# Columns of a modulation matrix by VectorE sums, low parts of early x tiles on GpSimd, and statistics' rows two tiles at a time, in a fused attention and mixer block

## The chip, the core and the metric

The kernel runs on one core of a Trainium2 chip, alone. The metric is the device time of one execution in microseconds (us). Engines are named as in the profile: PE (TensorE's matmuls, with PEld for its weight loads), DVE (VectorE), ACT (ScalarE), POOL (GpSimd), SP (the queue that issues most DMAs).

## The reference, cut to what matters

The input x has 2048 tokens of D = 448 channels; c is one row of 448 and w_mod is 448 x 2688.

```python
mod = (_silu(c) @ w_mod).reshape(c.shape[0], 6, 1, -1)
sa, ca, ga, sb, cb, gb = (mod[:, 0], mod[:, 1], mod[:, 2], mod[:, 3], mod[:, 4], mod[:, 5])
h = _layernorm(x, axis=-1) * (1 + ca) + sa
x = x + ga * _A_ref(h, A_wqkv, A_wo)     # linear attention: phi(k)^T v, then phi(q) times it, times wo
h = _layernorm(x, axis=-1) * (1 + cb) + sb
x = x + gb * _B_ref(h, B_w1, B_b1, B_w2, B_b2)   # layernorm, gelu MLP over the tokens
```

The change concerns the first layernorm with its scale `1 + ca` and shift `sa`, and the K projection behind it.

## The kernel before, in words

Tokens are cut into 16 tiles of 128 (t = 0 to 15), channels into four chunks of 128, 128, 128 and 64 (ch = 0 to 3; the last chunk is stored twice, in partitions 0 to 63 and 64 to 127). The order of the instructions on each engine is the order in which the program is written; a manual schedule is switched on, and semaphores are put in between engines.

A float32 product is made of float32r products of a rounded high part and the remaining low part. For tile t, `xt` is x transposed. ACT copies it into `hh` (`a_split_high`, L406), DVE subtracts to get `hl` (`a_split_low`, L409). The weights are scaled on the way: `1 + ca` is needed as a column, one number per channel on the partitions. ACT multiplies a chunk of the raw K weights `wr` by it into `wh` (`w_high`, L256), DVE makes the low part `wl` (`w_low`, L268). A tile's K projection `kp` is ten matmuls (`project`, L426): hh with wh, hh with wl, hl with wh for chunks 0 to 2, and hh with wh for chunk 3, where the doubled halves carry the low part. An eleventh matmul (`close`, L433) brings in the mean of the token and the shift: it uses rows that a small transpose (`a_transpose`, L399, tile `rw`) makes of the token statistics, which DVE lays out in `rowst` (`a_rows`, L389 and L391) and ACT copies into `hl` (`a_copy`, L402), and a weight row `wrow` (`row_out`, L290 and L291), which needs the sums of the scaled weights (`row_sum`, L283) and of the weights times `sa` (`row_part` on DVE, L274 and L276, into `accb`; `row_bias`, L286).

The columns come from `w_mod` in its own layout, channels of c on the partitions. For `1 + ca` (j = 1) two chunks are multiplied by silu(c) on PE (`col_mm`, L218 and L220), the others first weighted on DVE (`col_acc`, L204 to L211) and then summed by PE; `col_out` (L226) takes the column out of PSUM. For `sa` (j = 0) DVE weights all four pieces, PE sums once.

Statistics: for tiles 0 to 3 ACT makes the sums (L357, L336), for the others DVE does (`BN_STATS`, L373, and `BN_AGGR`, L374); GpSimd raises the variance to the powers 1/2 and -1/2 (L348, tile `mv`). The exp and relu of K on ACT (L440, L441), phi on DVE (`pk`, L446), its parts (`pkh` L504, `pkl` L506 or L508), the normalised x (`xn` L484, `xh` L488, `xl` L494) and the outer products (`cacc`, L530, eleven matmuls a tile) follow. From t = 4 on this is one loop; in an iteration t the parts of tile t + 3 are made, tile t + 1 is projected, and the outer product of tile t - 4 is added.

What the first 40 us wait for is loaded in the written order by SP; a DMA is issued when the one eight places earlier has landed.

Of the kernel before, what the change touches and what calls it, by code (L numbers as in the profile page):

```python
# [14 lines left out]
P = 128  # L15
# [13 lines left out]
RING = 6  # L29
# [3 lines left out]
DVE_LOW = (0, 1, 13, 14, 15)  # L33
# [8 lines left out]
WARM = 9  # L42
# [8 lines left out]
def block_kernel(ctx: ExitStack, tc: tile.TileContext, x, xt, wqkv, wo, w1, b1, w2, b2, c, wmod, wfirst, out):  # L51
# [47 lines left out]
    cst.tile([P, 40], F32, name="space")  # L99
# [19 lines left out]
    c_sb = cst.tile([P, 8], F32, name="c_sb")  # L119
    nc.sync.dma_start(c_sb, c)  # L120
# [12 lines left out]
    wm = {}  # L133
# [6 lines left out]
    raw_w = {}  # L140

    def load_qkv(j, new=None, chs=range(4)):
        new = new or slot
        for ch in chs:
            raw_w[j, ch] = new(f"wr{j}_{ch}")
            nc.sync.dma_start(raw_w[j, ch], wqkv[j, ch])

    def load_first(j):
        for k in range(4):
            w = D if k < 3 else 256  # L150
            wm[j, k] = slot(f"wm{j}_{k}", w)
            nc.sync.dma_start(wm[j, k], wfirst[j, :, k * D:k * D + w])
# [16 lines left out]
    load_qkv(0)  # L169
    load_xt(6)  # L170
    load_x(6)
    for t in (7, 8):
        load_xt(t)
        load_x(t)
# [11 lines left out]
    ec = cst.tile([P, 8], F32, name="ec")  # L186
    nc.scalar.activation(ec, c_sb, AF.Exp, scale=-1.0)
    sc = cst.tile([P, 8], F32, name="sc")
# [10 lines left out]
    one = ones[:, 0:1]  # L199

    def col_acc(j):
        acc = macc[j] = slot(f"acc{j}")
        if j:
            nc.vector.tensor_scalar_mul(acc, wm[j, 2], sc[:, 2:3])  # L204
        else:
            nc.vector.tensor_scalar_mul(acc, wm[j, 0], sc[:, 0:1])
            for k in (1, 2):
                nc.vector.scalar_tensor_tensor(acc, wm[j, k], sc[:, k:k + 1], acc, op0=ALU.mult, op1=ALU.add)
        for r, (c0, c1) in enumerate(((0, 256), (256, D))):
            p = slice(r * 64, (r + 1) * 64)  # L210
            nc.vector.scalar_tensor_tensor(acc[p, c0:c1], wm[j, 3][p, :c1 - c0], sc[p, 3:4], acc[p, c0:c1],  # L211
                                           op0=ALU.mult, op1=ALU.add)

    def col_mm(ps, a, b, first, last):
        b = b.to_broadcast([P, P])
        for ch in range(4):
            n = P if ch < 3 else 64
            nc.tensor.matmul(ps[:n, ch * P:(ch + 1) * P], a[:, ch * P:ch * P + n], b, start=first and ch == 0,  # L218
                             stop=last, skip_group_check=True)
        nc.tensor.matmul(ps[64:, 384:512], a[:, 384:D], b, start=False, stop=last, skip_group_check=True)  # L220

    def col_out(j, ps):
        col[j] = cst.tile([P, 4], F32, name=f"col{j}")
        ps = ps.rearrange("p (c n) -> p c n", n=P)[:, :, 0]
        if j == 1:
            nc.vector.tensor_scalar_add(col[j], ps, 1.0)  # L226
        else:
            nc.vector.memset(col[j], 0.0)
            nc.vector.tensor_copy(col[j][:, :3], ps[:, :3])
            nc.vector.tensor_copy(col[j][:64, 3:4], ps[:64, 3:4])  # L230

    def mod_part(j, k):
        if k == 0:
            macc[j] = (tslot if j == 5 else slot)(f"acc{j}", parts=G)
            nc.vector.tensor_scalar_mul(macc[j], wm[j, 0], sc[:G, 4:5])
        else:
            nc.vector.scalar_tensor_tensor(macc[j], wm[j, k], sc[:G, 4 + k:5 + k], macc[j], op0=ALU.mult, op1=ALU.add)
# [93 lines left out]
    heads, mv, xn = {}, {}, {}  # L331
# [18 lines left out]
    def a_stats_act(ts):  # L350
# [10 lines left out]
        def end():  # L361
            nc.gpsimd.tensor_scalar_mul(g[:, :, 0:1], sm[:, :, 0:1], 1.0 / D)
            nc.gpsimd.tensor_scalar(ve, sm[:, :, 2:3].to_broadcast([P, n, 2]), 1.0 / D, EPS,
                                    op0=ALU.mult, op1=ALU.add)
            a_pow(g, ve)
        return one, end

    def a_stats_dve(ts):
        g, ve = a_group(ts)

        def one(i):
            b6 = small.tile([P, 6], F32, name=f"st{ts[i]}", tag="st")
            nc.vector.bn_stats(b6, X[ts[i]])  # L373
            nc.vector.bn_aggr(mv[ts[i]][:, 0:2], b6)  # L374
# [4 lines left out]
        return one, end  # L379

    def a_stats(t):
        one, end = a_stats_dve((t,))
        one(0)
        end()

    def a_rows(t):
        r = rowst[t % RING]
        pair = mv[t][:, 0:2]
        nc.vector.tensor_copy(r[:, 64:].rearrange("p (b c) -> p b c", b=2)[:, :, 0:2],  # L389
                              pair.unsqueeze(1).to_broadcast([P, 2, 2]))  # L390
        nc.vector.tensor_sub(r[:, 66:68], pair, r[:, 64:66].bitcast(F32))  # L391
# [3 lines left out]
    def a_transpose(t0, n=1):  # L395
        ps = bank(f"rw{t0}")
        for i in range(n):
            tps[t0 + i] = ps[:, i * P:(i + 1) * P]
            nc.tensor.transpose(tps[t0 + i][:ROWS], rowst[(t0 + i) % RING][:, :ROWS].bitcast(F32), ident)  # L399

    def a_copy(t):
        nc.scalar.activation(heads[t][1][64:ROWS, 384:], tps.pop(t)[64:ROWS], AF.Copy)  # L402
# [5 lines left out]
    def a_split_low(t):  # L408
        nc.vector.tensor_sub(heads[t][1], XT[t], heads[t][0].bitcast(F32))  # L409
        XT[t] = None  # L410
# [27 lines left out]
    def a_exp(t, ps):  # L438
        eks[t] = (slot(f"ek{t}"), slot(f"rk{t}"))
        nc.scalar.activation(eks[t][0], ps, AF.Exp, scale=mv[t][:, 2:3])  # L440
        nc.scalar.activation(eks[t][1], ps, AF.Relu, scale=mv[t][:, 2:3])  # L441
# [79 lines left out]
    def a_outer(t):  # L521
# [4 lines left out]
        for ch in range(4):  # L526
            s = slice(ch * P, (ch + 1) * P)
            todo = [(xh, kh), (xh, kl)] + ([(xl, kh)] if ch < 3 else [])
            for i, (a, b) in enumerate(todo):
# [3 lines left out]
    pc = bank("col1")  # L533
    for k in range(2):
        col_mm(pc, wm[1, k], sc[:, k:k + 1], k == 0, False)
    nc.scalar.activation(sel_s, sel_f, AF.Copy)
    col_acc(1)
    a_split(0)
    col_mm(pc, macc.pop(1), one, False, True)
    keep_warm(5)  # L540
    col_out(1, pc)
    for ch in (3, 0, 1, 2):
        w_high(1, ch)
        w_low(1, ch)
    a_split(1)
    a_split(2)
    projects([(0, "hh", 0), (0, "hl", 0), (0, "hh", 3), (0, "hh", 1), (0, "hl", 1), (0, "wl", 0), (0, "hh", 2),
              (0, "hl", 2), (0, "wl", 1), (1, "hh", 0), (1, "hh", 1), (1, "hh", 2), (1, "hh", 3), (0, "wl", 2),
              (1, "wl", 0), (1, "wl", 1), (1, "wl", 2), (1, "hl", 0), (1, "hl", 1), (1, "hl", 2)], 1, "kp")
# [38 lines left out]
    project(4, 1, "kp")  # L588
    a_split(5)
    a_low(0)  # L590
    kps = [close(t, 1) for t in (0, 1)]
    a_transpose(2, 2)
    project(5, 1, "kp")
    a_exp(0, kps[0])
    a_pk(0, kps[0])
    dve45(1)
# [4 lines left out]
    a_exp(1, kps[1])  # L601
    a_norm(1)
    a_pk_parts(0)
    a_outer(0)
    a_pk(1, kps[1])
    a_rows(4)
    a_rows(5)
    a_transpose(4, 2)
    a_exp(2, kps[2])
    a_split_high(6)  # L610
    a_pk(2, kps[2])
    a_split_low(6)
# [6 lines left out]
    a_stats(6)  # L619
    a_pk_parts(1)  # L620
    a_low(1)
    a_rows(6)
    a_pk(3, kps[3])
    a_pk_parts(2)
    a_stats(7)
    wo_sb = []
    late = [t for t in range(NT) if t not in Q_EARLY.values()]
    for t in range(4, NT):
# [3 lines left out]
        if 4 < t < NT - 1:  # L632
            a_transpose(t + 1)
# [3 lines left out]
        if t > 4:  # L637
            a_outer(t - KV_LAG)
        if t in Q_EARLY:
# [3 lines left out]
        if 4 < t < NT - 2:  # L643
            a_rows(t + 2)
        if 5 <= t < 9:
            w_low(0, t - 5)
            row_part(0, t - 5)
        if 7 < t + 3 < NT:
            a_stats(t + 3)
        a_phi_q(t in Q_EARLY)  # L650
        if 4 < t < NT - 1:
            a_copy(t + 1)
        a_exp(t, kp)
# [4 lines left out]
        for i in highs[:1]:  # L658
            a_norm(i)
            a_high(i)  # L660
        a_pk(t, kp)
        if t + 3 < NT:
            a_split_low(t + 3)
        for i in highs[1:]:
            a_norm(i)
            a_high(i)
        for i in highs:
            a_low(i)
        if 4 <= t < 8:
# [564 lines left out]
def lay_out(inputs):  # L1234
# [12 lines left out]
    col = np.zeros((P, 8), c.dtype)  # L1247
    for k in range(3):
        col[:, k] = c[k * P:(k + 1) * P]
    col[:64, 3] = col[64:, 3] = c[3 * P:]  # L1250
    for k in range(4):
        col[:G, 4 + k] = c[k * G:(k + 1) * G]
    a['c'] = col
    a['B_wmod'] = a['w_mod']
    first = np.zeros((2, P, 3 * D + 256), c.dtype)
    for j in range(2):
        m = a['w_mod'][:, j * D:(j + 1) * D]
        for k in range(3):
            first[j, :, k * D:(k + 1) * D] = m[k * P:(k + 1) * P]
        first[j, :64, 3 * D:] = m[3 * P:, :256]  # L1260
        first[j, 64:, 3 * D:3 * D + 192] = m[3 * P:, 256:]
# [25 lines left out]
```

## Time and profile before, and how to read them

| what | value |
|---|---|
| median of 3 runs | 441.46 us (440.39, 441.46, 441.61) |
| the profiled execution: its time, and its span | 440.71 us, 439.0 us |
| PE busy | 433.3 us (99% of the span) |
| DVE busy | 364.0 us (83%) |
| ACT busy | 279.4 us (64%) |
| POOL busy | 118.2 us (27%) |
| granted TensorE clock | 1.00 in all stages |

The profile is of one execution. The span counts from its first to its last instruction; 1.7 us of the time lie around it. A row of the timeline gives start, duration, engine, source line, operation and tiles, how many instructions are merged in the row, and in brackets how long the engine had been idle and for whom. A row of the chain of waits gives start, duration, engine, tile and line; the chain is followed back from the last instruction to whatever released it. A row of the stages gives each engine's busy time in the stretch, the clock, the share of DMA time and the GB/s. In the groups, the first figure after the bar is the sum in us, the second the mean in ns.

### The profile page before, as it was taken

The numbers are of one execution on the slowest core, as the hardware profiler recorded it, in microseconds if no ns is written. First come the engines' busy times: TensorE is split into PE (matmuls) and PEld (weight loads), VectorE is DVE, ScalarE is ACT, GpSimd is POOL, SyncE is SP. The second block draws the span as 40 slices with busy tenths as digits, with TensorE's granted clock in tenths as the row PEclk, the third lists the DMA queues.
The fourth block names the chain that finished last, engine by engine and source line by source line (L and its number), as shares of the span: only waits on it lengthen the run. The fifth ranks groups of instructions, "written<-read, shape, count | busy, mean of one in ns | idle before, by whom it ended". The sixth has DMA issues, their size and how long they took to land.

```text
span 439.0 us, 7315 instructions
## 1 busy us (share of the span) xinstructions
PE 433.3 (99%) x2383; PEld 401.3 (91%) x2383; DVE 364.0 (83%) x822; ACT 279.4 (64%) x598; POOL 118.2 (27%) x200
## 2 busy tenths in 40 slices
PE   8999999999999999999999999999999999999996
PEld 7878899999899999999999999999999999999996
DVE  3989998689889999995579785829799988898894
ACT  3899877657676698885765263627555555655550
POOL 3137554300004567783300000010112231132010
PEclk9999999999999999999999999999999999999999
DMA  7997999545410025534616661579379987985430
GB/s 244 385 311 162 220 227 246 95 140 187 127 30 1 24 50 135 105 74 96 193 61 199 204 189 45 145 206 234 59 182 229 193 183 156 225 171 125 85 52 32
DMA packets 64085, 66.17 MB, mean 151 GB/s; under 512 B 4976, under 2 KB 55600, under 8 KB 64048
## 3 DMA queue, kind: packets, MB, share of 16 engines
q1 hardware_dynamic: 55120, 51.17, 38.3%
q0 software_dynamic: 8928, 14.55, 21.0%
q8 instruction: 18, 0.29, 0.3%
q14 instruction: 19, 0.16, 0.1%
HBM read 46.11 MB, written 7.34 MB: 122 GB/s over the span
## 4 chain that ended last, share of the span: by engine, by line
PE 96%; DVE 1%; ACT 1%; issue 0%; ACTq 0%
PE y L1077 19%; PE up L860 10%; PE up L861 10%; PE up L862 10%; PE y L1078 9%; PE op L810 8%; PE cacc L530 8%; PE qp L426 7%; PE kp L426 6%; PE tq L785 1%; PE col L218 1%; PE warm L181 1%; PE qp L433 1%; PE kvb L741 1%; PE rowb L283 1%; PE wp L877 1%
## 5 line engine op out<-in xcount | busy, mean ns | idle before, releaser
L860 PE MATMUL up<-h2h,ph 128*128 128x448 f32 x224 | 81.3, 363 | 0.0
L862 PE MATMUL up<-h2h,pl 128*128 128x448 f32 x224 | 81.1, 362 | 0.0
L861 PE MATMUL up<-h2l,ph 128*128 128x448 f32 x224 | 80.9, 361 | 0.0
L1032 POOL DMA_DIRECT2D a<-a x16 | 14.2, 963 | 139.4 <-DMA pr<-in_B_w_dram 75.3
L862 PEld LDWEIGHTS up<-h2h,pl 128*128 128x128 f32 x224 | 42.0, 188 | 3.1
L861 PEld LDWEIGHTS up<-h2l,ph 128*128 128x128 f32 x224 | 41.9, 187 | 3.1 <-DVE h2l L857 0.3
L860 PEld LDWEIGHTS up<-h2h,ph 128*128 128x128 f32 x224 | 42.0, 188 | 2.5
L83 DVE TENSOR_TENSOR pl<-pr,ph 128x512 fp32r<-128x512 f32 x46 | 30.8, 688 | 4.1 <-ACT ph L82 3.3
L1083 ACT ACTIVATE cc<-y 128x448 f32<-128x448 f32 x24 | 13.0, 546 | 26.8 <-PE y L1078 26.8
L82 ACT ACTIVATE ph<-pr 128x512 fp32r<-128x512 f32 x46 | 27.6, 624 | 0.8 <-PE up L862 0.5
L996 DVE TENSOR_TENSOR u<-u,mod 128x448 f32<-128x448 f32 x14 | 8.7, 623 | 21.6 <-ACT u L995 21.4
L530 PE MATMUL cacc<-pkh,xh 128*128 128x448 f32 x64 | 24.4, 382 | 0.3 <-ACT pkh L504 0.3
L810 PE MATMUL op<-wph,pth 128*128 128x448 f32 x64 | 24.5, 383 | 0.0
L995 ACT ACTIVATE u<-up,b1c 128x448 f32<-128x448 f32 x14 | 8.8, 625 | 24.1 <-PE up L862 23.5
L530 PE MATMUL cacc<-pkl,xh 128*128 128x448 f32 x64 | 23.3, 364 | 0.2 <-DVE pkl L506 0.2
L426 PE MATMUL kp<-wh,hh 128*128 128x448 f32 x64 | 23.2, 373 | 0.2 <-ACT wh L256 0.2
L426 PE MATMUL qp<-wh,hh 128*128 128x448 f32 x64 | 23.3, 364 | 0.0
L810 PE MATMUL op<-wpl,pth 128*128 128x448 f32 x64 | 23.1, 362 | 0.0
L1097 POOL DMA_DIRECT2D out_dram<-yt x14 | 12.5, 893 | 39.1 <-DVE yt L1088 29.7
L767 POOL TENSOR_SCALAR den<-den 128x16 f32<-128x16 f32 x16 | 8.8, 549 | 47.7 <-DVE den L764 47.7
L348 POOL TENSOR_TENSOR mv<-ve,roots 128x2 f32<-128x2 f32 (+1 forms) x13 | 12.5, 960 | 22.4 <-DVE ve L377 21.6
L1038 DVE TENSOR_TENSOR a<-a,s 128x512 f32<-128x512 f32 (+1 forms) x32 | 18.5, 619 | 0.0
(238 smaller groups left out, 1382.7 us busy)
## 6 DMA issues: line engine op xcount, KB each, us to landing
pr<-in_B_w_dram SPq DMA_DIRECT2D x56, 256.0 KB, 3.3
a<-in_B_w_dram SPq DMA_DIRECT2D x32, 256.0 KB, 4.8
a<-in_B_w_dram SPq DMA_DIRECT2D x32, 192.0 KB, 4.6
xt<-in_xt_dram SPq DMA_DIRECT2D x16, 256.0 KB, 4.9
x<-in_A_x_dram SPq DMA_DIRECT2D x16, 224.0 KB, 4.8
wm<-in_B_wmod_dram SPq DMA_DIRECT2D x16, 196.0 KB, 4.8
out_dram<-x SPq DMA_DIRECT2D x14, 224.0 KB, 2.2
out_dram<-yt POOLq DMA_DIRECT2D x14, 224.0 KB, 6.3
```

The costliest lines, as they stand in the source:

```text
L82: nc.scalar.activation(hi, full, AF.Copy)
L83: nc.vector.tensor_sub(lo, full, hi.bitcast(F32))
L426: nc.tensor.matmul(pps[t, j][:, :D], a[:, ch * P:(ch + 1) * P], w, start=first, stop=False)
L530: nc.tensor.matmul(cacc[ch][:, :D], a[:, s], b, start=(t == 0 and i == 0), stop=(t == NT - 1 and i == len(todo) - 1))
L810: nc.tensor.matmul(opb[t][:, :D], a, b, start=(n == 0), stop=(n == len(todo) - 1))
L860: nc.tensor.matmul(ps[:, :D], hi[:, sl], mh, start=first, stop=False)
L861: nc.tensor.matmul(ps[:, :D], hi[:, sl], ml, start=False, stop=False)
L862: nc.tensor.matmul(ps[:, :D], lo[:, sl], mh, start=False, stop=last)
L1032: nc.gpsimd.dma_start(w, a, accum_op=ALU.add)
L1038: nc.vector.tensor_tensor(w, raw2[q, a][i], raw2[q, b][i], op=op)
L1077: nc.tensor.matmul(ps[:, :D], h[:, s], w, start=opens and r == 0, stop=False, skip_group_check=True)
L1078: nc.tensor.matmul(ps[:, :HD], l[:, s], wh, start=False, stop=closes and r == PAIRS - 1, skip_group_check=True)
```

## The change

**Columns.** `w_mod`'s first two blocks are stored transposed and chunk by chunk (`wt`, 128 x 448, one column more for the 1 of `1 + ca`). PE spreads silu(c) once over all partitions into a PSUM bank (`spread`, tile `scr`); DVE then makes each chunk's column with one multiplication with an accumulated sum (`col_sum`). The matmuls of `col_mm` and DVE's `col_acc` and `col_out` go. The chunks' loads alternate with those of the K weights; the first two are issued by ACT. Both blocks together are 192 KB larger than before.

**Low parts.** GpSimd instead of DVE makes `hl` of tiles 0, 1, 2, 3, 5 and 6 (`POOL_LOW`).

**Rows.** Two tiles share one `rowst` and one transpose: each pair needs one pair of DVE operations instead of two, one transpose instead of two. Statistics from tile 8 on come in pairs, too. Those of tiles 2 and 3 move from ACT to DVE.

**Order.** The projections of tiles 0, 1, 3 and 4 take their products in another order; the outer products of tiles 0 and 1 take the low part of phi(k) last; `pkl` of tile 2 moves from ACT and a DMA to DVE.

```diff
-RING = 6
+RING = 3
-DVE_LOW = (0, 1, 13, 14, 15)
+DVE_LOW = (0, 1, 2, 13, 14, 15)
-WARM = 9
+WARM = 6
+POOL_LOW = (0, 1, 2, 3, 5, 6)
...
+    def load_first(j, ch, eng=nc.sync):
+        wt[j, ch] = slot(f"wt{j}_{ch}", D + 1)
+        eng.dma_start(wt[j, ch][:, :D], wfirst[j, ch])
+        nc.gpsimd.memset(wt[j, ch][:, D:], 1.0 if j else 0.0)
...
-    load_first(1)
+    load_first(1, 0, nc.scalar)
+    c_sb = cst.tile([P, 4], F32, name="c_sb")
+    nc.sync.dma_start(c_sb, c)
     load_xt(0)
-    load_qkv(1, chs=(3, 0, 1, 2))
-    load_xt(1)
+    load_qkv(1, chs=(0,), eng=nc.scalar)
+    for ch in range(1, 4):
+        load_first(1, ch)
+        load_qkv(1, chs=(ch,))
+        if ch == 1:
+            load_xt(1)
     load_xt(2)
-    load_first(0)
     load_x(0)
+    load_x(1)
+    for ch in range(4):
+        load_first(0, ch)
     load_xt(3)
-    load_x(1)
...
+    def spread():
+        for k in range(4):
+            nc.tensor.matmul(scr[:, k * G:(k + 1) * G], sc[:G, k:k + 1].to_broadcast([G, P]), ident[:G, :G],
+                             start=(k == 0), stop=(k == 3), skip_group_check=True)
+        nc.tensor.matmul(scr[:, D:D + 1], ones[:1], ones[:1, :1], start=False, stop=True, skip_group_check=True)
+
+    def col_sum(j, ch):
+        if j not in col:
+            col[j] = cst.tile([P, 4], F32, name=f"col{j}")
+            if j == 0:
+                nc.gpsimd.memset(col[j], 0.0)
+        p = slice(0, 64 if j == 0 and ch == 3 else P)
+        w = wt.pop((j, ch))[p]
+        nc.vector.scalar_tensor_tensor(w, w, 1.0, scr[p, :D + 1], op0=ALU.mult, op1=ALU.mult,
+                                       accum_out=col[j][p, ch:ch + 1])
...
     def a_rows(t):
-        r = rowst[t % RING]
-        pair = mv[t][:, 0:2]
-        nc.vector.tensor_copy(r[:, 64:].rearrange("p (b c) -> p b c", b=2)[:, :, 0:2],
-                              pair.unsqueeze(1).to_broadcast([P, 2, 2]))
-        nc.vector.tensor_sub(r[:, 66:68], pair, r[:, 64:66].bitcast(F32))
+        g, r = groups.pop(t)[:, :, 0:2], rowst[t // 2 % RING].rearrange("p (t b c) -> p t b c", t=2, b=2)
+        nc.vector.tensor_copy(r[:, :, :, 0:2], g.unsqueeze(2).to_broadcast([P, 2, 2, 2]))
+
+        def low():
+            nc.vector.tensor_sub(r[:, :, 0, 2:4], g, r[:, :, 0, 0:2].bitcast(F32))
+        return low
...
     def a_split_low(t):
-        nc.vector.tensor_sub(heads[t][1], XT[t], heads[t][0].bitcast(F32))
+        eng = nc.gpsimd if t in POOL_LOW else nc.vector
+        eng.tensor_sub(heads[t][1], XT[t], heads[t][0].bitcast(F32))
         XT[t] = None
```

Three places show what stands on an engine now. First PE, from its start (`warm` are matmuls whose result nobody reads; the number behind a name is the buffer's). Before:

```order
L181 MATMUL warm<-ones 128x128 x9
L218 MATMUL col_203<-sc,wm_0_118 128x128 x3
L218 MATMUL col_203<-sc,wm_0_118 64x128
L220 MATMUL col_203<-sc,wm_0_118 64x128
L218 MATMUL col_203<-sc,wm_1_120 128x128 x3
```

and now:

```order
L184 MATMUL warm<-ones 128x128 x6
L207 MATMUL scr<-ident,sc 128x112 x4
L209 MATMUL scr<-ones 128x1
L184 MATMUL warm<-ones 128x128 x4
L417 MATMUL kp_245<-wh_0_220,hh_215 128x448
L417 MATMUL kp_245<-wh_0_220,hl_216 128x448
L417 MATMUL kp_245<-wl_0_222,hh_215 128x448
L417 MATMUL kp_245<-wh_1_224,hh_215 128x448
```

Behind the `spread` of silu(c) nothing of the columns is left on PE, and the first tile's products go chunk by chunk.

Second POOL, behind its first memsets. Before it had nothing but the small steps of the statistics there (`as` and `ve` are sums and variances, `mv` the result):

```order
L362 TENSOR_SCALAR mv_293<-as_295 128x2
L363 TENSOR_SCALAR ve_294<-as_295 128x4
L348 TENSOR_TENSOR mv_293<-ve_294,roots 128x2x2
L362 TENSOR_SCALAR mv_368<-as_370 128x2
L363 TENSOR_SCALAR ve_369<-as_370 128x4
L348 TENSOR_TENSOR mv_368<-ve_369,roots 128x2x2
L348 TENSOR_TENSOR mv_363<-ve_364,roots 128x2x2
```

and now (`hl_216`, `230`, `242`, `307`, `386`, `408` are the low parts of tiles 0, 1, 2, 3, 5, 6; `mv_280`, `335`, `346` the statistics of tiles 0 and 1, 2 and 3, 4 and 5):

```order
L400 TENSOR_TENSOR hl_216<-xt_115,hh_215 128x512
L400 TENSOR_TENSOR hl_230<-xt_124,hh_229 128x512
L400 TENSOR_TENSOR hl_242<-xt_136,hh_241 128x512
L215 MEMSET col_286 128x4
L351 TENSOR_SCALAR mv_280<-as_282 128x2
L352 TENSOR_SCALAR ve_281<-as_282 128x4
L337 TENSOR_TENSOR mv_280<-ve_281,roots 128x2x2
L400 TENSOR_TENSOR hl_307<-xt_154,hh_306 128x512
L337 TENSOR_TENSOR mv_335<-ve_336,roots 128x2x2
L400 TENSOR_TENSOR hl_386<-xt_164,hh_385 128x512
L400 TENSOR_TENSOR hl_408<-xt_168,hh_407 128x512
L337 TENSOR_TENSOR mv_346<-ve_347,roots 128x2x2
```

Six operations of 128 x 512 stand between the steps of the statistics.

Third DVE, from the last `row_part` (`accb`) on. Before:

```order
L276 SCALAR_TENSOR_TENSOR accb_333<-wr_3_128,col_329,accb_333 128x448
L389 CAST rowst_104<-mv_293 128x2x2
L391 TENSOR_TENSOR rowst_104<-mv_293,rowst_104 128x2
L389 CAST rowst_106<-mv_293 128x2x2
L391 TENSOR_TENSOR rowst_106<-mv_293,rowst_106 128x2
L409 TENSOR_TENSOR hl_358<-xt_158,hh_357 128x512
L484 TENSOR_SCALAR xn_361<-x_148,mv_293 128x448
L373 BN_STATS st_365<-x_160 128x6
L374 BN_AGGR mv_363<-st_365 128x2
L291 TENSOR_TENSOR wrow_291<-rowb_311,wrow_291 2x448
```

and now:

```order
L380 CAST rowst_104<-mv_280 128x4x2
L265 SCALAR_TENSOR_TENSOR accb_310<-wr_2_129,col_286,accb_310 128x448
L383 TENSOR_TENSOR rowst_104<-mv_280,rowst_104 128x2x2
L265 SCALAR_TENSOR_TENSOR accb_310<-wr_3_134,col_286,accb_310 128x448
L477 TENSOR_SCALAR xn_333<-x_138,mv_280 128x448
L365 BN_STATS st_337<-x_156 128x6
L365 BN_STATS st_339<-x_158 128x6
L368 BN_AGGR mv_335<-st_337 128x2
L368 BN_AGGR mv_335<-st_339 128x2
L371 TENSOR_SCALAR ve_336<-mv_335 128x4
L400 TENSOR_TENSOR hl_331<-xt_160,hh_330 128x512
L280 TENSOR_TENSOR wrow_278<-rowb_292,wrow_278 2x448
```

The rows of tiles 0 and 1 stand between the pieces of `accb` now, so the last two pieces come after the statistics of those tiles; the statistics of tiles 2 and 3 stand ahead of the low part of tile 4 (`hl_331`) and of `wrow`.

More of the change, by code (lines that the diff above doesn't have):

```diff
@@ L198, in block_kernel @@
     col = {}
[L199 to L230, printed above, removed]
+    scr = bank("scr")
+    def spread():
[12 more added lines that the diff above has]
+                                       accum_out=col[j][p, ch:ch + 1])
     def mod_part(j, k):
@@ L369, in a_stats_dve, with first, second @@
         g, ve = a_group(ts)
[L371 to L374, printed above, removed]
+        b6 = {}
+        def first(i):
+            b6[i] = small.tile([P, 6], F32, name=f"st{ts[i]}", tag="st")
+            nc.vector.bn_stats(b6[i], X[ts[i]])
+        def second(i):
+            nc.vector.bn_aggr(mv[ts[i]][:, 0:2], b6[i])
         def end():
@@ L618, in block_kernel @@
     kps.append(close(4, 1))
-    a_stats(6)
+    first, second, end = a_stats_dve((6, 7))
+    first(0)
+    first(1)
+    second(0)
+    second(1)
+    end()
     a_pk_parts(1)
     a_low(1)
-    a_rows(6)
     a_pk(3, kps[3])
     a_pk_parts(2)
-    a_stats(7)
     wo_sb = []
@@ L666, in block_kernel @@
             a_high(i)
+        if pair:
+            first(1)
         for i in highs:
             a_low(i)
+        if pair:
+            second(1)
+            end()
         if 4 <= t < 8:
@@ L1246, in lay_out @@
     c = a['c'].reshape(D)
[L1247 to L1252, printed above, removed]
+    col = np.zeros((P, 4), c.dtype)
+    col[:G] = c.reshape(4, G).T
     a['c'] = col
     a['B_wmod'] = a['w_mod']
-    first = np.zeros((2, P, 3 * D + 256), c.dtype)
+    first = np.zeros((2, 4, P, D), c.dtype)
     for j in range(2):
[L1257 to L1261, printed above, removed]
+        m = a['w_mod'][:, j * D:(j + 1) * D].T
+        for ch in range(3):
+            first[j, ch] = m[ch * P:(ch + 1) * P]
+        first[j, 3, :64] = first[j, 3, 64:] = m[3 * P:]
     a['first'] = first
```

188 lines of the change are left out of this document (101 added, 87 removed).

## The prediction

> **What bounds the kernel now.** I read the page's totals first, then the stages, then the chain of waits, and last the single instructions of the stage in which PE waits. The page says that PE is busy for nearly the whole span and makes up nearly the whole chain:
>
> ```profile
> span 439.0 us, 7315 instructions
> PE 433.3 (99%) x2383; PEld 401.3 (91%) x2383; DVE 364.0 (83%) x822; ACT 279.4 (64%) x598; POOL 118.2 (27%) x200
> PE 96%; DVE 1%; ACT 1%; issue 0%; ACTq 0%
> ```
>
> So time can only come from matmuls taken off PE, or from stretches in which PE stands still. The stages (stretch and length, then busy us of PE, PEld, DVE, ACT and POOL, clock, DMA share, GB/s) show where it does:
>
> ```profile
> 10.72:17.01 6.29, 6.29 (x32) 5.87 (x33) 6.09 (x12) 5.20 (x12) 0.00 (x0) 1.00 1.06 387
> 17.01:24.68 7.67, 7.67 (x42) 6.29 (x42) 6.61 (x21) 6.94 (x21) 3.14 (x6) 1.00 1.05 382
> 24.68:28.97 4.29, 3.76 (x18) 2.56 (x17) 3.86 (x10) 3.94 (x9) 1.13 (x1) 1.00 1.08 307
> 28.97:37.18 8.21, 7.82 (x39) 6.63 (x39) 7.49 (x24) 7.81 (x17) 4.00 (x6) 1.00 0.78 209
> 37.18:60.00 22.82, 22.82 (x114) 20.40 (x115) 21.55 (x60) 21.05 (x42) 13.85 (x16) 1.00 0.98 215
> 60.00:130.00 70.00, 70.00 (x366) 63.71 (x365) 57.88 (x127) 47.71 (x96) 12.07 (x17) 1.00 0.57 145
> ```
>
> From 37.18 on PE is busy all the time; ahead of it DVE and ACT are over 90% busy too, and the transfers run at up to 387 GB/s. The chain (start, duration, what) says what PE's last wait was for:
>
> ```profile
> 9.44 1.24 ACT wh L256 x2
> ...
> 10.72 6.28 PE kp L426 x30
> 17.01 0.92 PE col L218 x7
> ...
> 18.04 1.58 PE rowb L283 x7
> ...
> 36.52 0.61 DVE hl L409
> 37.13 0.04 issue
> 37.18 1.88 PE kp L426 x8
> ...
> 39.26 0.11 PE rw L399
> ```
>
> At 37.18 PE takes up the low part of tile 7, which DVE finished at 37.13. Whatever PE gains earlier is lost unless DVE reaches that instruction earlier. So **the end moves by as much as DVE's low part of tile 7 moves, plus the matmuls removed behind it**.
>
> **The change, part by part.**
>
> *The start.* Before, the first projection stands at 10.72, behind the whole column. Now the first chunk is enough: the weights' first chunk is the third transfer, wh takes 0.62 us (two in 1.24) and the column's sum is one DVE instruction. Its nearest rows are the residual's sum from PSUM, 0.62 us and 0.08 for reading the accumulator (sum and mean ns behind the bar):
>
> ```profile
> L819 DVE SCALAR_TENSOR_TENSOR x<-op,x 128x448 f32<-128x448 f32 x16 | 9.9, 618 | 0.0
> L819 DVE DVE_READ_ACCUMULATOR x<-op,x 128x1 f32 x16 | 1.3, 84 | 0.0
> ```
>
> I take 0.70 a chunk; 0.62 and 0.78 are its bounds. I put PE's first projection at about 7.7. That is 3 us early, but it is not the gain: the next chunks hold PE up. What arrives when is read from two ACT instructions that waited for transfers, and from the last steps of the statistics of tiles 0 and 1:
>
> ```profile
> 7.66 0.63 ACT L406 ACTIVATE hh<-xt 128x512 fp32r<-128x512 f32 x1 [3.50 <-DMA xt<-in_xt_dram]
> 14.43 0.58 ACT L357 ACTIVATE junk<-x 128x448 f32<-128x448 f32 x1 [1.02 <-DMA x<-in_A_x_dram]
> 16.55 0.56 ACT L357 ACTIVATE junk<-x 128x448 f32<-128x448 f32 x1
> 18.05 0.19 ACT L336 ACTIVATION_READ_ACCUMULATOR junk<-x,as 128x1 f32 x1
> 18.60 1.06 POOL L348 TENSOR_TENSOR mv<-ve,roots 128x4 f32<-128x4 f32 x1
> ```
>
> The first came after 1056 KB of loads, the second after 3488 KB: 359 KB per us. In the new order 2080 KB end with the last chunk of w_mod for the scale, so it lands at 7.66 + 1024/359 = 10.5. The last sum is over at about 11.45 (0.7 us, after the low part ahead of it), wh of chunk 3 at 12.1, hh of tile 2 at 12.6, wrow at 13.2. The statistics of tiles 0 and 1 took ACT 1.7 us each (16.55 to 18.24, the second): they end at 16.5 instead of 18.24. GpSimd's steps behind them took 1.42 (to 19.66), so mv is there at 17.9 instead of 19.66: **1.75 us early**. On PE the block of column matmuls between 17.01 and 18.04 goes, 1.03 us, but PE then waits for rows and bias.
>
> *Low parts on GpSimd.* No GpSimd operation with two full inputs is in the trace. The nearest rows are its selects, the rows that show what it does to DVE stand beside them:
>
> ```profile
> 1.07 0.29 POOL masks.py:199 TENSOR_SCALAR_AFFINE_SELECT ident<-ident 128x128 f32<-128x128 f32 x1
> 2.62 0.67 POOL L97 TENSOR_SCALAR_AFFINE_SELECT mask<-mask 112x448 f32<-112x448 f32 x1
> 2.66 0.65 DVE L189 TENSOR_SCALAR ec<-ec 128x8 f32<-128x8 f32 x1 [1.58 <-ACT ec L187]
> 3.35 0.20 DVE L190 RECIPROCAL ec<-ec 128x8 f32<-128x8 f32 x1
> 150.16 0.68 DVE L829 SCALAR_TENSOR_TENSOR y<-x,nm,mod 128x448 f32<-128x448 f32 x1
> 150.27 0.66 POOL L824 TENSOR_SCALAR nm<-sm 128x1 f32<-128x1 f32 x1
> ```
>
> From 128 to 448 elements a select grows by 0.38 us, 1.2 ns an element: 0.77 us for 512. That is the low end if a second input costs nothing; twice as much, 1.5 us, is the high end if both inputs are read in turn. I take 0.78, nearest to the row, against 0.61 on DVE (the chain's row of hl).
>
> The same rows show **the two engines shutting each other out**. A DVE operation on 8 elements, begun 0.04 us into the select, took 0.65 us and ended with it (3.31 against 3.29). The other way round, GpSimd's step on one element at 150.27 took 0.66 us and ended 0.09 after DVE's two-input operation. So I charge DVE the length of a GpSimd low part wherever DVE would start an operation with two SBUF inputs. [...]
>
> Where it falls: hl of tiles 0 and 2 lies beside column sums and transfers and costs nothing; without that cover it is one length, 0.78, each. That of tile 1 delays one wl by 0.15 us (counted above). That of tile 3 starts with mv at 17.9, just as DVE wants to lay out rows: DVE gets on at 18.7. Then rows, `accb` twice and the subtraction of the rows, 1.6 us by their groups (0.68 for `accb`, 0.17 for a small one, less 0.08 of overlap each): the last `accb` ends at 20.3. Before:
>
> ```profile
> 18.80 2.12 DVE L276 SCALAR_TENSOR_TENSOR accb<-wr,col,accb 128x448 f32<-128x448 f32 x3
> 32.57 0.63 DVE L506 SCALAR_TENSOR_TENSOR pkl<-pk,pkh 128x448 fp32r<-128x448 f32 x1 [0.48 <-ACT pkh L504]
> L389 DVE CAST rowst<-mv 128x4 fp32r<-128x4 f32 x16 | 2.7, 166 | 0.0
> 24.93 0.69 DVE L409 TENSOR_TENSOR hl<-xt,hh 128x512 fp32r<-128x512 f32 x1 [0.33 <-DMA xt<-in_xt_dram]
> L374 DVE BATCH_NORM_AGGREGATE mv<-st 128x2 f32<-128x6 f32 x12 | 2.2, 182 | 0.4
> L373 DVE BATCH_NORM_STATS2 st<-x 128x6 f32<-128x448 f32 x12 | 7.5, 622 | 0.0
> ```
>
> it ended at 20.92, so 0.6 of the 1.75 us are left.
>
> *DVE's list from the last `accb` to the low part of tile 7.* Before, 20.92 to 37.13: 16.2 us. It loses: two low parts (tiles 5 and 6), 1.2; rows, from fourteen small operations to six, 0.9; one small operation of the variance, 0.1; two waits, 0.8 (the brackets in the rows of pkl and of the low part of tile 5); the wait between statistics and their aggregate where two tiles are interleaved, 0.3. It gains: statistics of tiles 2 and 3, 0.62 twice, their aggregates 0.18 twice and a small one, together 1.75, and pkl of tile 2, 0.54. Net: -1.0, so 15.2. GpSimd's hl of tile 5 starts when the statistics of tiles 2 and 3 are raised to their powers; DVE does the low part of tile 4 and wrow meanwhile, 1.2 us against 1.06 of the power, and wants to lay out the rows 0.1 us later: 0.7 us of standstill. That of tile 6 comes beside statistics, one SBUF input, and I take it as covered. If not, it is 0.78. So tile 7's low part ends at 20.3 + 15.2 + 0.7 = 36.2, **0.9 us early**.
>
> *Transposes.* Behind that point nine transposes of rows become four; each holds PE 0.11 us: -0.55 us.
>
> *At nothing:* ACT's loss of the statistics of tiles 2 and 3, since DVE's list is longer (if ACT held the end, two tiles at 1.7 us sooner at most); issuing two loads on ACT, which waits for their data anyway (the 3.50 us in its row); pairs of statistics later on, where PE is never late between 60 and 130. If that cover were gone, an iteration would wait for one statistic, 0.6 us.
>
> **The sum:** -0.9 - 0.55 = -1.5 us (rounded). The profiled execution took 440.71 us, its span 439.0 and 1.7 around it: 439.2. It was 0.75 below the median of the runs, 441.46, from which the same sum gives 440.0. I put the forecast at **439.5**, between both.
>
> **The rivals.**
>
> *No shutting out.* If DVE's two-input operations run beside GpSimd's, the standstills at tiles 3 (0.8) and 5 (0.7) go: -3.0 us, 438.0. Against it stands the 0.65 us row; for it, that no row shows it for a two-input operation, and that DVE's `accb` at 18.80 ran beside GpSimd's power at 18.60 without delay.
>
> *A long hold, slower.* Both inputs are read in turn, 1.5 us a low part, and DVE is shut out for all of it. Then tiles 3 and 5 cost 0.74 more each, tile 6 is no longer covered (0.7), and tile 1 pushes the last columns, statistics and mv by 0.65: 2.8 us more, +1.3 us, 442.3. The place is DVE between 18 and 27 us; each 0.1 us of length costs nearly 0.4, so the change loses from 1.2 us on. For it: the high end of my own bound, and a DVE that is over 90% busy. Against it: a length of twice the select's.
>
> *No gain at the middle length.* At 1.1 to 1.2 us the standstills eat what the rest brings: -0.3 us, 440.8 against the mean of both bases.
>
> *The change does not do what it says.* The first chunks come late, since they share the transfers with loads issued at the same time. If the last chunk for the scale landed 1.5 us later, the lead at mv would be gone: 0 us, 441.0.
>
> **How the numbers follow.** A measurement of this kernel can tell about 0.3%, 1.3 us, from no change. Forecast case (0.78 us, shut out): 0.42, with its own range of 438.6 to 440.6; its middle is just over 0.3%, so I count 0.27 of it as faster and 0.15 as the same. No shutting out: 0.23, faster. Middle length: 0.17, the same. Long hold: 0.12, slower. Late chunks: 0.06, 0.05 the same and 0.01 slower. So faster 0.50, the same 0.37, slower 0.13. The range reaches into both outer cases: 437.4 to 442.0.
>
> **What would show it right or wrong.** In the new profile: the first projection on PE near 7.7; a sum of a column at 0.7 us; GpSimd's low part 0.8 us long, and DVE operations with two inputs that are longer than 0.7 beside it; mv of tiles 0 and 1 ready at 17.9; the last `accb` at 20.3; the low part of tile 7 at 36.2, with PE busy throughout behind it. If GpSimd's low parts take 1.2 us or more and DVE's rows wait for them, the forecast is too low; if DVE's operations beside them keep their 0.6 to 0.7 us, it is too high. If PE still stands still behind tile 7, the sum's frame is wrong.

## The result and the profile after

The changed kernel takes 441.34 us (median of 14 runs), the kernel before 440.77 beside it: a ratio of 1.0004, 95% interval 0.9993 to 1.0015. (The ratio is worked out from the single runs; the quotient of the two medians is 1.0013.) That is no difference that can be measured, where a gain of 0.4% was forecast. The profiled execution took 441.38 us. In the experiments below, one execution of e3 (713 us) and one of s1 (605 us), at mean clocks of 0.56 and 0.66, are left out of the ratios.

First the page's span and totals: 109 instructions fewer (7206 for 7315) stand in a span that is 0.7 us longer.

```profile
span 439.7 us, 7206 instructions
PE 430.2 (98%) x2337; PEld 397.9 (90%) x2337; DVE 362.7 (82%) x805; ACT 275.0 (63%) x587; POOL 122.0 (28%) x204
```

The stages of before, now (columns as there: busy us of PE, PEld, DVE, ACT, POOL, then clock, DMA share, GB/s), and PE's longest waits (total, times, longest):

```profile
17.01:24.68 7.67, 6.49 (x27) 4.25 (x25) 6.42 (x14) 3.58 (x8) 4.34 (x4) 1.00 1.06 384
24.68:28.97 4.29, 2.41 (x7) 2.20 (x8) 4.19 (x9) 2.66 (x7) 1.80 (x2) 0.67 1.07 288
28.97:37.18 8.21, 8.18 (x39) 7.09 (x39) 6.89 (x21) 6.59 (x15) 3.35 (x3) 0.97 0.63 183
37.18:60.00 22.82, 22.82 (x114) 20.02 (x113) 20.67 (x53) 20.36 (x42) 11.41 (x12) 1.00 0.92 195
```

```profile
PE rw L389 <- DVE rowst L383: 2.0, 1, 2.0
PE kp L417 <- DVE wl L257: 1.3, 1, 1.3
```

In the stage from 24.68 on PE is busy for 2.41 us where it had 3.76, and the granted clock, 1.00 before, is 0.67. The single wait of 2.0 us is new. GpSimd's and DVE's rows around it (start, duration) say why:

```profile
5.75 1.27 POOL L400 TENSOR_TENSOR hl<-xt,hh 128x512 fp32r<-128x512 f32 x1 [1.22 <-ACT hh L396]
...
18.04 1.26 POOL L400 TENSOR_TENSOR hl<-xt,hh 128x512 fp32r<-128x512 f32 x1
24.00 2.49 POOL L400 TENSOR_TENSOR hl<-xt,hh 128x512 fp32r<-128x512 f32 x2
```

```profile
6.35 0.62 DVE L218 SCALAR_TENSOR_TENSOR wt<-wt,scr 128x449 f32<-128x449 f32 x1 [2.40 <-PE scr L209]
...
9.12 1.48 DVE L257 SCALAR_TENSOR_TENSOR wl<-wr,col,wh 128x448 fp32r<-128x448 f32 x1
...
18.09 1.25 DVE L380 CAST rowst<-mv 128x8 fp32r<-128x8 f32 x1 [0.94 <-POOL mv L337]
...
19.96 0.68 DVE L265 SCALAR_TENSOR_TENSOR accb<-wr,col,accb 128x448 f32<-128x448 f32 x1
...
24.06 1.23 DVE L380 CAST rowst<-mv 128x8 fp32r<-128x8 f32 x1 [0.24 <-POOL mv L337]
25.33 1.18 DVE L383 TENSOR_TENSOR rowst<-mv,rowst 128x4 fp32r<-128x4 f32 x1
...
37.78 0.68 DVE L400 TENSOR_TENSOR hl<-xt,hh 128x512 fp32r<-128x512 f32 x1
```

A low part takes GpSimd 1.26 us. The column sum at 6.35, one of whose inputs is `scr` in PSUM, keeps its 0.62 beside that of tile 0. Beside that of tile 1 the low part of a weight chunk (9.12) lasts 1.48 us, where the one ahead of it took 0.68; PE's wait of 1.3 us is for this one. Beside that of tile 3 the cast of eight elements lasts 1.25 us and ends with it (19.34 against 19.30); beside those of tiles 5 and 6 the cast and the low half of the next rows last 1.23 and 1.18, one behind the other. The chain (start, duration, what) shows what follows on PE:

```profile
24.06 1.25 DVE rowst L380
...
25.33 1.19 DVE rowst L383
...
26.56 0.45 PE rw L389
27.01 3.24 PE kp L417 x10
```

The ten products of tile 5 take 3.24 us; ten such products take 2.0 to 2.1 later on. The low part of tile 7 ends at 38.46, 1.34 us later than before (37.12).

### The profile page after: what moved, and what is told of

The parts are those of the page before. It is cut to its first block, busy times and chain, and to the rows that moved or that the text cites. A ratio compares the mean times of both kernels' runs of the same rounds, so it can differ in the third digit from the quotient of the medians.

```text
span 439.7 us, 7206 instructions
## 1 busy us (share of the span) xinstructions
PE 430.2 (98%) x2337; PEld 397.9 (90%) x2337; DVE 362.7 (82%) x805; ACT 275.0 (63%) x587; POOL 122.0 (28%) x204
## 4 chain that ended last, share of the span: by engine, by line
PE 93%; DMA 4%; DVE 1%; SPq 0%; POOL 0%; issue 0%; POOLq 0%
PE y L1101 19%; PE up L884 10%; PE up L885 10%; PE up L886 10%; PE y L1102 9%; PE op L834 8%; PE cacc L523 8%; PE qp L417 7%; PE kp L417 5%; DMA wt<-in_first_dram 2%; DMA xt<-in_xt_dram 2%; PE tq L809 1%; PE qp L424 1%; PE kvb L765 1%; PE wp L901 1%; PE kp L424 1%
## 5 line engine op out<-in xcount | busy, mean ns | idle before, releaser
L417 PE MATMUL kp<-wh,hh 128*128 128x448 f32 x64 | 24.3, 388 | 0.4 <-ACT wh L245 0.4
L523 PE MATMUL cacc<-pkl,xh 128*128 128x448 f32 x56 | 20.3, 362 | 0.0
L417 PE MATMUL kp<-wl,hh 128*128 128x448 f32 x48 | 17.9, 377 | 1.4 <-DVE wl L257 1.3
```

Of the source, the lines that this page charges most:

```text
L417: nc.tensor.matmul(pps[t, j][:, :D], a[:, ch * P:(ch + 1) * P], w, start=first, stop=False)
```

## The experiments

**Theory A:** a low part on GpSimd shuts VectorE out for its whole 1.26 us; those of tiles 5 and 6 hold the rows of tiles 2 and 3, PE stands, and a lower clock comes behind it. **Theory B**, the rival: VectorE's own longer list (statistics of tiles 2 and 3, one more low part of phi) eats the gain. Ratios are to the kernel before, run on the same chip. Differences below come from medians; where two runs come from different chips, their ratios can give a difference some 0.3 us smaller or larger.

**e1: tiles 5 and 6 back on VectorE.**

```diff
-POOL_LOW = (0, 1, 2, 3, 5, 6)
+POOL_LOW = (0, 1, 2, 3)
```

> The changed kernel with the low parts of tiles 5 and 6 back on VectorE (GpSimd keeps those of tiles 0 to 3). Theory A (a low part of 1.26 us on GpSimd shuts VectorE out for its whole length; those of tiles 5 and 6 hold the rows of tiles 2 and 3 one after the other, and PE's 2.0 us of standstill and the lower clock behind it follow): the cast and the low half of these rows take about 0.17 us each, PE's wait for the rows falls from 2.0 to under 0.5 us, the granted clock stays at 1.00 between 24.7 and 29, and the low part of tile 7 ends near 36.4 to 37 in spite of two more operations of 0.6 on VectorE. Time: 1.5 us below the changed kernel, near 439.5, a ratio to the kernel before of 0.997. Theory B (VectorE's own longer list eats the gain: statistics of tiles 2 and 3, and one more low part of phi): two low parts more on VectorE, 1.2 us later, near 442 to 442.5, a ratio of 1.003 to 1.004.

439.45 us, ratio 0.9963 (0.9950 to 0.9976). A stage and the low part of tile 7:

```profile
24.68:28.97 4.29, 3.63 (x17) 2.73 (x17) 4.19 (x12) 3.52 (x8) 0.38 (x1) 1.00 1.08 300
```

```profile
35.81 0.68 DVE L400 TENSOR_TENSOR hl<-xt,hh 128x512 fp32r<-128x512 f32 x1
```

The clock stays, and tile 7's low part ends at 36.49, 1.97 us earlier, though VectorE has two low parts more to do. As theory A had it; B is out as the main cause.

**e2: every low part on VectorE.**

```diff
-POOL_LOW = (0, 1, 2, 3, 5, 6)
+POOL_LOW = ()
```

> The changed kernel with every low part on VectorE, so that of the change the columns, the rows in pairs and the moved statistics are left. Theory A: the hold at tile 3 (about 1.1 us on the cast of the rows of tiles 0 and 1) goes too, and the one beside the weight of chunk 1 (0.8 us); four low parts more on VectorE fall where it waits for transfers, all but that of tile 3. Near 439, a ratio to the kernel before of 0.996. Theory B: up to six low parts more at 0.6 us on VectorE, of which at least three are not hidden: 443 or more, a ratio of 1.004 or more.

438.49 us, ratio 0.9944 (0.9932 to 0.9957), half a microsecond better than theory A's figure. Rows and low part of tile 7:

```profile
23.08 0.17 DVE L380 CAST rowst<-mv 128x8 fp32r<-128x8 f32 x1 [0.24 <-POOL mv L337]
23.29 0.17 DVE L383 TENSOR_TENSOR rowst<-mv,rowst 128x4 fp32r<-128x4 f32 x1
...
34.78 0.68 DVE L400 TENSOR_TENSOR hl<-xt,hh 128x512 fp32r<-128x512 f32 x1
```

So the rest of the change saves 2.4 us (440.88 to 438.49), and the six low parts on GpSimd cost 2.85 (438.49 to 441.34): 1.9 of it tiles 5 and 6, 0.96 tiles 0 to 3.

**e4: the low parts alone, in the kernel before.**

```diff
+POOL_LOW = (0, 1, 2, 3, 5, 6)
...
-        nc.vector.tensor_sub(heads[t][1], XT[t], heads[t][0].bitcast(F32))
+        eng = nc.gpsimd if t in POOL_LOW else nc.vector
+        eng.tensor_sub(heads[t][1], XT[t], heads[t][0].bitcast(F32))
```

> The kernel before with only the low parts of tiles 0, 1, 2, 3, 5 and 6 moved to GpSimd; columns, rows and statistics as before. Theory A: each of them takes about 1.26 us, those of tiles 3, 5 and 6 shut VectorE out of rows or of accb, and the time goes up by 1 to 2 us: near 442.3, a ratio of 1.003. Theory B: VectorE is relieved of operations of 0.6 us, and the time goes down by up to 1 us: near 440, a ratio of 0.998.

442.40 us, ratio 1.0034 (1.0021 to 1.0048). GpSimd's low parts (count, then busy us and mean ns, then the idle time before them and what ended it), that of tile 5, and a piece of the chain:

```profile
L411 POOL TENSOR_TENSOR hl<-xt,hh 128x512 fp32r<-128x512 f32 x6 | 8.2, 1377 | 11.1 <-ACT hh L407 11.1
```

```profile
25.95 1.28 POOL L411 TENSOR_TENSOR hl<-xt,hh 128x512 fp32r<-128x512 f32 x1 [2.28 <-ACT hh L407]
```

```profile
26.01 1.24 DVE rowst L392
```

An operation on two elements, 0.16 us elsewhere, begins 0.06 us into it and holds the chain for 1.24. The low parts cost 1.5 us here too, without the rest of the change. That is less than the 2.85; here PE's longest wait for rows is 0.6 us, and the run's clock is 0.999.

**e3: PE kept busy in the standstill.** The six matmuls are unread.

```diff
     def a_transpose(t):
         ps = bank(f"rw{t}")
+        if t == 2:
+            for _ in range(6):
+                nc.tensor.matmul(ps[:, 256:384], ones, ones, start=True, stop=True)
```

> The changed kernel with six matmuls that nobody reads (128 by 128, fp32, into unused columns of the same bank) ahead of the transpose of the rows of tiles 2 and 3: PE is busy in the 2.0 us in which it waits for these rows. If the lower clock behind the standstill costs PE time that the end sees: clock 1.00 between 25 and 30, the ten products of tile 5 in 2.0 us instead of 3.24, and 1.2 us less in all, near 440.1, a ratio to the kernel before of 0.998. If VectorE's low part of tile 7, at 38.46, sets the end whatever PE did before it: the products are faster, but the time stays at that of the changed kernel, 441.3, a ratio of 1.000.

440.12 us, ratio 0.9978 (0.9969 to 0.9987). The stage, and the ten products of tile 5 in the chain:

```profile
24.68:28.97 4.29, 3.61 (x22) 3.18 (x21) 4.15 (x11) 2.65 (x6) 1.41 (x2) 1.00 1.06 295
```

```profile
26.48 2.04 PE kp L420 x10
```

DVE's rows are shut out as before (1.24 and 1.18 us), but PE's wait falls to 0.7 us, the clock stays and 1.2 us come back. So the standstill costs twice: its own length, and, where the clock falls behind it, the lower clock. Two other executions of e3 have a mean clock of 0.995 and take no longer (440.1 and 440.3 us): where the clock falls matters, as the next run shows.

**a2: the changed kernel once more.**

> The changed kernel once more, unaltered, as the base of this group of runs and to see a second profile of it. If the half clock behind PE's standstill is what its time hangs on: the clock falls below 0.7 between 25 and 29 us again and the time is near 441.3; or it stays at 1.00 and the time is near 440.0. If the clock falls and the time is still near 440, the clock is not what parts the runs.

441.39 us, ratio 0.9996 (0.9982 to 1.0010). The execution profiled here took 440.04 us, 1.34 less than the one above, with the same 2.0 us of standstill. Two stages, PE's early wait and tile 7:

```profile
10.72:17.01 6.29, 6.29 (x25) 5.71 (x24) 4.70 (x14) 5.43 (x14) 2.46 (x5) 0.73 1.06 385
...
24.68:28.97 4.29, 2.71 (x14) 2.48 (x15) 4.15 (x11) 2.66 (x7) 1.51 (x2) 1.00 1.07 296
```

```profile
10.35 0.47 PE L417 MATMUL kp<-wl,hh 128*128 128x448 f32 x1 [1.79 <-DVE wl L257]
```

```profile
36.32 0.68 DVE L400 TENSOR_TENSOR hl<-xt,hh 128x512 fp32r<-128x512 f32 x1
```

Here the clock falls after the early wait for wl, 1.79 us long, and not behind the rows; PE makes the loss up before 24.68 (7.23 us busy between 17.01 and 24.68, where the first profile had 6.49). Tile 7's low part ends at 37.00. Of the 26 executions of the changed kernel three kept a mean clock of 1.0 and took 439.8 to 440.1 us; the 23 at 0.995 or 0.996 form two groups, 7 at 440.0 to 440.9 and 16 at 441.2 to 442.0. The two profiles are one of each group; that the others fall the same way is inferred. The expectation, which knew one place for the lower clock, had only half of it.

**d1, d2: subtractions on GpSimd that nobody reads,** in the kernel of e2, behind the power of tiles 2 and 3.

```diff
...
     end23()
+    nc.gpsimd.tensor_sub(dum3, ones.unsqueeze(1).to_broadcast([P, 4, P]), ident.unsqueeze(1).to_broadcast([P, 4, P]))
```

> The kernel that had every low part on VectorE, 438.5, with one subtraction more on GpSimd (128 by 512, two inputs in SBUF, its result unread), right behind the power of tiles 2 and 3, where the changed kernel has the low part of tile 5. Nothing waits for it. Theory A (VectorE is shut out for its whole length): it takes 1.26 us, the cast of the rows takes about 1.2 instead of 0.17, and the time goes up by 0.9 to 1.0, to 439.4. Theory B (what counts is VectorE's own list or the late result of GpSimd's low parts): an operation that nobody waits for costs nothing, 438.5.

439.90 us, ratio 0.9969 (0.9957 to 0.9980). The subtraction, VectorE's rows, the stage and PE's two waits in it:

```profile
23.39 1.30 POOL L579 TENSOR_TENSOR dum<-ones,ident 128x512 f32<-128x512 f32 x1
```

```profile
23.45 1.27 DVE L382 CAST rowst<-mv 128x8 fp32r<-128x8 f32 x1 [0.24 <-POOL mv L339]
24.75 0.16 DVE L385 TENSOR_TENSOR rowst<-mv,rowst 128x4 fp32r<-128x4 f32 x1
```

```profile
24.68:28.97 4.29, 3.43 (x11) 2.83 (x12) 4.15 (x13) 2.43 (x6) 0.01 (x1) 0.75 1.09 307
```

```profile
25.06 0.29 PE L391 MATMUL rw<-ident,rowst 128*98 128x128 f32 x1 [1.12 <-DVE rowst L385]
26.31 0.47 PE L419 MATMUL kp<-wh,hl 128*128 128x448 f32 x1 [0.48 <-DVE hl L402]
```

An operation without a reader or a dependence on VectorE stretches the cast from 0.17 to 1.27 us and costs 1.4 (1.1 by the ratios, as the chips differ). Neither VectorE's list nor a late result can do that. This execution, 440.79 us, has the lower clock too, behind a standstill of 1.1 us and one of 0.5 us shortly after; the other six, at 0.999 or 1.0, took 439.7 to 440.0.

> The same with two such subtractions one behind the other. Theory A: the cast waits for the first and the low half of the rows for the second, each about 1.2 us, PE stands for some 2 us at the transpose, and the time goes up by 2 to 3, to 440.5 to 441.7, the upper end if the clock falls as well. Theory B: 438.5.

Two of them: 439.94 us, ratio 0.9981 (0.9968 to 0.9993), which can't be told from one. Theory A's figure and its account of the low half were wrong here, and the rows say why (the execution profiled took 441.52 us):

```profile
25.02 1.31 POOL L580 TENSOR_TENSOR dum<-ones,ident 128x512 f32<-128x512 f32 x1
```

```profile
25.00 0.16 DVE L385 TENSOR_TENSOR rowst<-mv,rowst 128x4 fp32r<-128x4 f32 x1
25.08 0.62 DVE L367 BATCH_NORM_STATS2 st<-x 128x6 f32<-128x448 f32 x1
25.83 1.65 DVE L402 TENSOR_TENSOR hl<-xt,hh 128x512 fp32r<-128x512 f32 x2
```

The second subtraction (it may wait for the first, since both write dum) starts 0.02 us after the low half, which so keeps its 0.16. By these rows, who starts first has the way. The statistics beside it, one input, are not held (0.62); the two low parts behind them are, by 0.38 (1.65, where e2's pair took 1.27). Four of the twelve executions, at a clock of 0.996, took 441.2 to 441.5; the others 439.6 to 440.3.

**d3: memsets in the same place,** which write but read nothing.

```diff
...
     end23()
+    nc.gpsimd.memset(dum, 0.0)
+    nc.gpsimd.memset(dum, 0.0)
```

> The same place with two memsets of 128 by 1024 on GpSimd, about 0.95 us each, which write and read nothing. If only GpSimd's reading shuts VectorE out: the rows take their 0.17 us, 438.5. If any GpSimd operation does: cast and low half take up to 0.9 us each, and the time goes up by 1 to 1.6, to 439.5 to 440.1.

439.47 us, ratio 0.9959 (0.9945 to 0.9974): 1.0 above e2 (0.7 by the ratios), the lower end of the second expectation, but with the cast alone held. The memsets and the rows:

```profile
23.11 0.95 POOL L578 MEMSET dum<- 128x1024 f32 x1
24.11 0.95 POOL L579 MEMSET dum<- 128x1024 f32 x1
```

```profile
23.19 0.90 DVE L381 CAST rowst<-mv 128x8 fp32r<-128x8 f32 x1 [0.24 <-POOL mv L338]
24.12 0.16 DVE L384 TENSOR_TENSOR rowst<-mv,rowst 128x4 fp32r<-128x4 f32 x1
```

The first memset held the cast to its own end (24.09 against 24.06), but the second did not hold the two-input operation, which began 0.01 us into the second memset and took its 0.16. So the cast was held by a GpSimd operation that only writes, too (0.90 us for 0.17); that the two-input operation was not (0.16) rests on this one row and its 0.01 us.

**r1: rows tile by tile again,** in the kernel of e2.

```diff
...
     def a_rows(t):
-        g, r = groups.pop(t)[:, :, 0:2], rowst[t // 2 % RING].rearrange("p (t b c) -> p t b c", t=2, b=2)
-        nc.vector.tensor_copy(r[:, :, :, 0:2], g.unsqueeze(2).to_broadcast([P, 2, 2, 2]))
+        groups.pop(t)
+        for i in (t, t + 1):
+            r = rowst[i % RING]
+            pair = mv[i][:, 0:2]
...
     def a_transpose(t):
         ps = bank(f"rw{t}")
+        for i in range(2):
...
```

> The kernel that had every low part on VectorE, 438.5, with the rows laid out tile by tile again (four small VectorE operations and two transposes for each pair of tiles, where the pairs have two and one). The prediction's own terms: five transposes more behind the low part of tile 7, 0.55 us, and eight to ten small operations more ahead of it, 0.6 to 0.9: 439.6 to 440. If pairs of rows bring nothing because VectorE has slack there: 439.0 (the transposes alone).

440.11 us, ratio 0.9982 (0.9973 to 0.9991). Its low part of tile 7:

```profile
36.30 0.69 DVE L403 TENSOR_TENSOR hl<-xt,hh 128x512 fp32r<-128x512 f32 x1
```

It ends at 36.99, 1.5 later than in e2. Pairs of rows save 1.6 us, near the 1.45 that the prediction's two terms for them add up to. Their split is another: 1.5 lies ahead of the end of that low part (0.9 in the prediction), and 0.4 behind it, by the spans of the two profiles (0.55).

**s1: statistics of tiles 2 and 3 on ScalarE,** in the kernel of e2.

```diff
-    first23, second23, end23 = a_stats_dve((2, 3))
-    first23(0)
-    first23(1)
-    second23(0)
-    second23(1)
+    act23, end23 = a_stats_act((2, 3))
+    act23(0)
+    act23(1)
     end23()
```

> The same kernel with the statistics of tiles 2 and 3 on ScalarE again. If VectorE's longer list is what costs (theory B): its list is 1.75 us shorter, and the time falls by about 1, to 437.5. If what counts is when the rows of tiles 2 and 3 are there: ScalarE takes 1.7 us a tile where VectorE takes 0.85, the rows come 1 to 2 us later, PE waits for them, and the time goes up by 1 to 1.7, to 439.5 to 440.2, more if the clock falls.

437.93 us, ratio 0.9930 (0.9916 to 0.9944). Rows and tile 7:

```profile
22.41 0.17 DVE L380 CAST rowst<-mv 128x8 fp32r<-128x8 f32 x1
...
34.11 0.68 DVE L400 TENSOR_TENSOR hl<-xt,hh 128x512 fp32r<-128x512 f32 x1
```

Theory B's direction: 0.56 us less. The rows come at 22.41 and not at 23.08, since ScalarE starts the statistics at 17.29 and VectorE reaches them at 20.00. Moving them to VectorE cost 0.6 us, a fifth of what GpSimd's low parts cost.

**b1 and v1.** b1 is e2 with the statistics of tile 4 behind the first phi; v1 is b1 with s1's edit.

```diff
     low()
-    first45(0)
-    second45(0)
...
+    first45(0)
     first45(1)
+    second45(0)
     second45(1)
     end45()
```

> The same kernel with one thing moved: the statistics of tile 4 (0.75 us on VectorE between the rows of tiles 2 and 3 and the low part of tile 5, for which PE waits 0.48 us) stand beside those of tile 5, behind the first phi. If the chain through this low part, the first phi and its high half (PE resumes with it at 27.20) sets the end: 0.4 to 0.7 us less, 437.8 to 438.1. If the low part of tile 7 at the end of VectorE's list sets it, whose length is the same: 438.5.

> The best of the runs put together: every low part on VectorE, the statistics of tiles 2 and 3 on ScalarE, those of tile 4 beside tile 5's, behind the first phi. If the two gains (0.56 and 0.39 us) are two, VectorE's shorter list and the earlier first phi: 437.5. If they are one, because both only bring the first phi forward: 437.9, that of the better one alone.

b1: 438.10 us, ratio 0.9933 (0.9920 to 0.9947); by medians 0.4 below e2, but the intervals overlap. v1: 437.78 us, ratio 0.9926 (0.9913 to 0.9940), 0.15 below s1, which can't be told from nothing. The two gains are mostly one: tile 7's low part begins in b1 at 34.53, in v1 at 34.17 and in s1 at 34.11.

```profile
34.53 0.68 DVE L400 TENSOR_TENSOR hl<-xt,hh 128x512 fp32r<-128x512 f32 x1
```

```profile
34.17 0.68 DVE L400 TENSOR_TENSOR hl<-xt,hh 128x512 fp32r<-128x512 f32 x1
```

e2, s1, b1 and v1 all beat both kernels.

## Why the prediction was wrong in its size, step by step

The time fell inside the range, but not by the forecast case: it lies 1.8 us above 439.5, beyond the forecast case's own 438.6 to 440.6. The range held it because it had been stretched towards the long hold, which had a chance of 0.12. The mechanism that the text described, VectorE shut out by GpSimd's low parts, was there; its size and its reach were not as in the sum.

- **The frame held.** "The end moves by as much as DVE's low part of tile 7 moves, plus the matmuls removed behind it": the span less the end of that low part is 401.88 us before (439.0 less 37.12), and 401.24, 401.30, 401.21, 401.14 and 401.30 in the changed kernel, a2, e1, e2 and d3. The transposes are part of this step of 0.6 to 0.7 (forecast 0.55): e4, with the transposes of before, has 401.83, and r1, with two for each pair again, 401.51, so they account for 0.3 to 0.4 of it; what the rest is stays open.
- **The start held.** First projection 7.74 (forecast 7.7), a column sum 0.62 and 0.08 (0.70), mv of tiles 0 and 1 at 18.06 (17.9), the last `accb` at 20.64 (20.3).
- **The length of a low part failed.** "I take 0.78": it is 1.26, past the 1.2 us from which the text itself said that the change loses. The select that the value came from reads one tensor; its row could not price a second input (and gives 0.75 rather than 0.77 for 512 elements), and the high end of the bound, 1.5, was nearer than 0.78. The 1.1 to 1.2 us of the rival at the middle length are the author's estimate; no run shows a low part of that length, the six took 1.27 us in the mean. The low part of tile 1, too, held `wl` by 0.80 us, not 0.15; mv came on time all the same.
- **"That of tile 6 ... I take it as covered" failed.** It followed tile 5's without a gap and held the low half of the rows for 1.18 us. The standstills on VectorE were 1.08, 1.06 and 1.02 us at tiles 3, 5 and 6 (durations less 0.17, 0.17 and 0.16), 3.2 us instead of the 1.5 in the sum. With a low part at 1.26 the prediction's own slope, 0.4 us for 0.1, gives +0.4 and not -1.5. That this is close to the measured +0.6 is luck: the slope knows no clock, and a2's profile, which lost nothing to the clock behind the rows, lies 0.7 below the profile of before.
- **The charge was put too narrowly.** VectorE was charged only for operations with two SBUF inputs; that was the author's assumption, and no row of before shows that two are needed. The operation that was hit first, twice, is a cast with one (1.25 and 1.23 us for 0.17). The sum put the standstills of tiles 3 and 5 at these casts all the same, since that is where rows are laid out.
- **The clock was missing.** No step asked what a standstill of 2 us does to PE's clock. Tile 5's ten products took 3.24 instead of 2.0 us; the exponentials, the phis and tile 7's low part followed. a2's profile is the sum without that: 440.04 us, 0.84 above the forecast of 439.2 for the profiled execution. Of the 1.34 between the two profiles 0.3 is that a2's rows were laid out earlier (23.76 for 24.06); that the rest is the clock fits the 1.2 us of e3.
- **The parts that brought something:** rows in pairs 1.6 us (r1, forecast 1.45), the moved statistics a loss of 0.6 (s1, forecast within VectorE's list). What is left of e2's 2.4 us, some 1.4, falls to the columns, the transfers and the changed order by difference; no run measured these alone.

So a gain of 2.4 us was there, and 2.85 us were given back by six operations that were moved to an engine with time to spare.

## What to carry to other kernels

An operation moved from VectorE to GpSimd may not leave VectorE: where VectorE came to a cast or an operation with two SBUF inputs beside a low part of GpSimd's, that operation lasted longer, by 0.80 us at tile 1 and by 1.08, 1.06 and 1.02 at tiles 3, 5 and 6, for a low part that takes 0.61 to 0.69 on VectorE itself. An operation with one input in PSUM (the column sum beside tile 0's low part, 0.62) and the statistics beside d2's second subtraction (0.62) were not held, so those are the places to look for. Price a moved operation by a row with the same number of inputs, and if there is none, give both ends of the bound the same weight. Where a change adds a standstill of the matmul engine, look at the granted clock of the stage behind it as well as at the wait.

## What the hardware showed beyond that

PE's clock fell behind standstills of 2.0 us (0.67 in the mean over 24.68 to 28.97, 0.50 from 27 to 29), of 1.8 us (a2, 0.73 in the mean over 10.72 to 17.01) and of 1.1 us with 0.5 us shortly after (d1, 0.75 over 24.68 to 28.97). Other standstills as long brought no fall: a2's 2.0 us (1.00 over 24.68 to 28.97), and the 1.3 us for `wl` in the first profile (1.00 over 10.72 to 17.01). The rows of a2 (two microseconds each) show the clock at 0.50:

```profile
10.00:12.00 2.00, 1.65 (x6) 1.52 (x7) 1.86 (x5) 1.13 (x3) 0.00 (x0) 0.77 1.05 391
12.00:14.00 2.00, 2.00 (x6) 1.77 (x6) 0.76 (x2) 1.94 (x6) 1.32 (x2) 0.50 1.07 387
14.00:16.00 2.00, 2.00 (x10) 1.82 (x9) 2.00 (x9) 1.91 (x8) 0.23 (x1) 0.88 1.05 382
```

What parts the standstills with a fall from those without, no run here shows.
